# Attention with four score banks and early products in runs of twelve, and three expert chunks loaded through the later pool

## The chip, the core and the metric

The kernel runs as one program on one core of a Trainium2 chip. The metric is the device time of an execution in microseconds. The time of the kernel before is the median of three runs: 646.68 us (645.85 to 648.88).

The core has five engines with a queue each. TensorE (PE) multiplies matrices and writes only to PSUM, a memory of eight banks, each 128 partitions by 512 float32. ScalarE (ACT) and VectorE (DVE) read PSUM and work elementwise; GpSimd (POOL) works on SBUF only and issues gathers and scatters; SyncE (SP) issues most DMA transfers. An engine takes its instructions in the order of its queue, and waits at the first whose inputs are not there.

## The reference, cut to what matters

The computation is an attention with a window, a gated pair of products, and a layer of eight experts:

```python
# attention: q, k, v of (batch 2, heads 8, sequence 768, head dim 64)
scores = scale * np.matmul(q, k.transpose(0, 1, 3, 2))
keep = (pos[None, :] < n_sink) | ((rel >= 0) & (rel < window))   # n_sink 4, window 128
scores = np.where(keep, scores, -1e9)
a = np.exp(scores - scores.max(-1, keepdims=True))
a = a / (a.sum(-1, keepdims=True) + 1e-9)
x = np.matmul(a, v)                       # then as (1536 tokens, 512)
# gated product
x = ((x @ w_a) * (x @ w_b)) @ w_out       # w_a, w_b: 512 x 1536; w_out: 1536 x 512
# experts: each token goes to one of 8, at most 192 tokens per expert, best logits first
logits = x @ w_gate
for e in range(8):
    h = np.maximum(x[assigned == e] @ w1[e], 0.0)     # 512 x 1024
    out[assigned == e] = h @ w2[e]                    # 1024 x 512
```

## The kernel before, in words

**Exactness.** The products run in a float32 format of reduced mantissa (F32R). Where that is not enough, a value is split into a high part and the low rest, and a product becomes three: high by high, high by low, low by high. So xh and xl are the two parts of the attention's output, whi and wlo those of a weight, ehi and elo those of an expert's weight.

**Attention.** It is worked off in 24 steps (n = 0 to 23): two batches, three groups g of two query blocks each, four pairs of heads hp. The order of the instructions on PE, ACT, DVE and POOL is written out by hand: the framework adds the semaphores, but moves nothing on these four engines. One round of the loop in `attention` works on four steps at once:

- `turned` and `turned_low` (L231 to L255) turn k and q of step n+2 on PE into one bank; ACT writes the high part of T, DVE the low part.
- `scores` (L257 to L280) makes the scores of step n+1, in two groups j = 0, 1 of two heads. Each head has a bank of its own from a ring `s`, which has two (SB = 2). Three matmuls fill it; DVE reduces it with the mask (L277), ACT takes the exponential (L279).
- `factors`, `normed`, `sinks` (L282 to L317) norm the weights of step n, on DVE and POOL. Where g > 0, the eight sink columns are put into a tile AS of their own.
- `weights_turned` (L328) turns the weights of step n for each head, into a ring `at` of three banks; `sinks_turned` (L319) turns AS into the third bank of the same ring. Where g = 0 there are no sinks and `sinks_turned` does nothing.
- `copied` (L337), one round later, copies these banks to SBUF: the first head and the sinks (ast) on ACT, the second head on DVE.
- `values` (L352) multiplies them by v into one bank px, and ACT copies xh from it; `values_low` lets DVE write xl from px and xh.

Between these stand places 0 to 6, at each of which `fill` may put other work into the queues: idle matmuls (`busy`), the conversion of the first weights from 64-bit words (rounds 7 to 14, `PACE`), and **early products**. These are the gated products of the first two blocks of w_a and w_b with the first two thirds of the attention's output: eight banks, each the sum of twelve matmuls of 512 columns (L470), into one bank `pa` of a pool of its own, and evacuated by ACT (L476) or DVE (L478). `FILL` says how many stand at each place of a round: two at place 0, one at each of places 3 to 6, from round 9 on; what is left comes after the loop.

The order of a round on PE before: turn (n+2), two early products, scores j = 0 (n+1), values (n-1), scores j = 1 (n+1), one early product, weights (n) of the first head, one, of the second head, one, sinks (n), one. The eight PSUM banks are: `s` 2, turn 1, `at` 3, px 1, `pa` 1.

**After the attention** come the gated products (L559), the product with w_out (`second`, L977) with the routing of the tokens (`routing`) between its parts, and the experts. `second` makes twelve blocks of 128 tokens; each is stored to the DRAM tensor x2d by a DMA that ACT issues (L984), the last one stays in SBUF as x2last. `first_rows` (L1009) gathers the first expert's tokens from x2d by two DMAs of POOL (L1018); they must follow the eleventh store. PE turns the gathered rows (L1035), adds the rows of x2last (L1147), and starts the first expert (L1092).

**The experts' weights** come in 64 chunks of 512 KB, eight per expert, each loaded by a DMA of SP (`weight_load`, L997) into a tile eraw, from which ACT makes ehi and DVE elo. Chunks 0 to 3 are loaded into the pool `exraw` (three buffers) long before they are needed, and converted at the end of the routing. The later pool `more` (six buffers) lies in memory that `second` uses until its end. `load` (L1072) decides which pool a chunk takes; before, chunks below 7 take `exraw`. A chunk's load stands in SP's queue behind that of the chunk before.

Of the kernel before, what the change touches and what calls it, by code (L numbers as in the profile page):

```python
# [9 lines left out]
F32 = mybir.dt.float32  # L10
F32R = mybir.dt.float32r
# [6 lines left out]
PSUM = bass.MemoryType.PSUM  # L18
# [21 lines left out]
WARM = 12  # L40
BUSY = {(-2, 0): 7, (-1, 0): 1, (-1, 1): 1, (-1, 3): 1, (0, 0): 1, (0, 1): 1, (0, 3): 1, (2, 4): 3, (7, 0): 1}
CONV_IN = 2
FILL = (2, 0, 0, 1, 1, 1, 1)
FILL1 = (2, 0, 0, 1, 1, 1, 1)
PACE = (1, 1, 1, 0, 0, 0, 1)
ORDER = (0, 1, 0)
SINKV = (0, 2)
FIRST = (("q", 0, 0, 2), ("k", 0, 0, 2), ("q", 0, 2, 4), ("k", 0, 2, 4), ("v", 0, 0, 2), ("q", 0, 4, 8), ("k", 0, 4, 8),
         ("v", 0, 2, 4), ("q", 1, 0, 4), ("k", 1, 0, 4), ("v", 0, 4, 8), ("q", 1, 4, 8), ("k", 1, 4, 8), ("s", 0), ("v", 1))
# [1 line left out]
         8: (("w", 3),), 9: (("v", 3), ("s", 1), ("q", 4), ("k", 4)), 13: (("v", 4), ("q", 5), ("k", 5)), 14: (("v", 5),)}  # L51
CONV_AT = (7, 9, 11, 13)
CONV_ON = (0, 0, 0, 0, 1)
SB, ATB = 2, 3
SINK = 8
WB, AB, NB, FB = 4, 2, 1, 2
KB = 128 + SINK
# [6 lines left out]
def f32(ap):  # L64
    return ap.bitcast(F32)


class Kernel:
# [110 lines left out]
    def open_attention(self, ctx):  # L179
        tc = self.tc  # L180
        self.qkp = ctx.enter_context(tc.tile_pool(name="qkp", bufs=3))
        self.kt = ctx.enter_context(tc.tile_pool(name="kt", bufs=1))
        self.aw = ctx.enter_context(tc.tile_pool(name="aw", bufs=3))
        self.atps = ctx.enter_context(tc.tile_pool(name="atps", bufs=1, space=PSUM))
        self.raw, self.vb, self.T, self.vs, self.vraw = {}, {}, {}, {}, {}
        self.AS = [self.kt.tile([128, 2, 128], F32R, name=f"AS{n}") for n in range(3)]
        self.nAS = 0
        for AS in self.AS:
            self.nc.gpsimd.memset(f32(AS), 0.0)

    def busy(self, n):

        if n:
            p = self.abe.tile([128, 512], F32, name="none", tag="pa", bufs=1)
            for _ in range(n):
                self.nc.tensor.matmul(p[:, 0:256], self.idle[:, 0:128], self.idle[:, 0:256], start=True, stop=True)

# [59 lines left out]
    def scores(self, st, j):  # L257
        nc, b, g, hp = self.nc, st.b, st.g, st.hp
        i = 2 * g + j
        if j == 0:  # L260
            st.A2 = self.aw.tile([128, 2, 2, 256 + SINK], F32, name="A", tag="A", bufs=4)
            st.r2 = self.aw.tile([128, 2, 2], F32, name="rs", tag="rs", bufs=4)
        T = self.T[b, hp]
        flat = T.rearrange("p t k c -> p t (k c)")
        c0 = KB if i == 0 else 0
        lo, n = (0, 128) if i == 0 else (KB * (i - 1), 256 + SINK)
        mask = self.mask0 if i == 0 else self.mask1 if i == 1 else self.mask2
        col0 = ((b * 6 + i) * self.H) + 2 * hp
        for h in range(2):
            s = self.atps.tile([128, 256 + SINK], F32, name="s", tag="s", bufs=SB)  # L270
            hs = slice(64 * h, 64 * h + 64)
            for t, (tq, tk) in enumerate(((0, 0), (0, 1), (1, 0))):
                nc.tensor.matmul(s[:, :n], T[hs, tq, 6 + i % 2, 0:128], flat[hs, tk, lo:lo + n],  # L273
                                 start=(t == 0), stop=(t == 2))
            sm = self.aw.tile([128, 256 + SINK], F32, name="sm", tag="sm", bufs=4)
            cc = slice(col0 + h, col0 + h + 1)
            nc.vector.tensor_tensor_reduce(out=sm[:, :n], in0=s[:, :n], in1=mask, scale=-self.scale, scalar=BIG,  # L277
                                           op0=OP.add, op1=OP.min, accum_out=self.negmax[:, cc])
            nc.scalar.activation(st.A2[:, j, h, c0:], sm[:, :n], AF.Exp, bias=self.negmax[:, cc], scale=-1.0,  # L279
                                 accum_out=self.sums[:, cc])  # L280
# [38 lines left out]
    def sinks_turned(self, st):  # L319
        nc = self.nc  # L320
        if not st.g:
            return
        pt = self.atps.tile([128, 2, 128], F32R, name="pt", tag="at", bufs=ATB)
        for n in range(2):
            nc.tensor.transpose(pt[:, n, :], st.AS[:, n], self.identr)
        st.ps.append((pt[0:6 * SINK], None))
# [25 lines left out]
    def values(self, st):  # L352
        nc, D, b, g, hp = self.nc, self.D, st.b, st.g, st.hp
        i0 = 2 * g
        px = self.atps.tile([128, 512], F32, name="px", tag="px", bufs=1)[:, 0:256]
        if g:
            nc.tensor.matmul(px, self.vs[b][:, hp, :], st.ast.rearrange("p a b -> p (a b)"), start=True, stop=False,
                             skip_group_check=True)
        vcol = [slice((2 * hp + h) * D, (2 * hp + h + 1) * D) for h in range(2)]
        parts = [(i0, slice(0, 256), slice(1, 3))]  # L360
        if g:
            parts.append((i0 - 1, slice(0, 128), slice(0, 1)))
        parts.append((i0 + 1, slice(128, 256), slice(3, 4)))
        for n, (kb, cols, sl) in enumerate(parts):
            for h in range(2):
                vv = self.vb[b, kb].rearrange("p h d -> p (h d)")
                nc.tensor.matmul(px[64 * h:64 * h + 64, cols], vv[:, vcol[h]],  # L367
                                 st.AT[h][:, sl].rearrange("p a b -> p (a b)"),
                                 start=(not g and n == 0), stop=(n == len(parts) - 1), skip_group_check=True)
        st.px = px  # L370
        nc.scalar.activation(st.out[0][:, hp, :], px, AF.Copy)
# [2 lines left out]
        xh, xl = [x[:, st.hp, :] for x in st.out]  # L374
        self.nc.vector.tensor_tensor(xl, st.px, f32(xh), op=OP.subtract)

    def attention(self, XH, XL, wpool, GE, abe):

        steps = []
        for gi in range(6):  # L380
            b, g = divmod(gi, 3)
            cols = slice(256 * (gi % 2), 256 * (gi % 2) + 256)
            for hp in range(4):
                steps.append(SimpleNamespace(b=b, g=g, hp=hp, AT=[], ps=[],
                                             out=(XH[gi // 2][:, :, cols], XL[gi // 2][:, :, cols])))
        early = self.early(wpool, XH, XL, GE, abe)

        done, raw, under_way = [0], {}, {}

        def fill(n, place):  # L390
            self.busy(BUSY.get((n, place), 0))
            for i, n1 in enumerate(CONV_AT):
                if (n, place) == (n1, 0):
                    engs = [(self.nc.vector, self.nc.gpsimd)[e] for e in CONV_ON]
                    under_way[i] = self.split_steps(wpool, raw.pop(i), engs[:4], engs[4])
                if n >= n1 and i in under_way:
                    for _ in range(7 if (n, place) == (n1 + CONV_IN - 1, 6) else PACE[place]):
                        res = next(under_way[i], None)
                        if res:
                            self.ahead[i // 2].append(res)  # L400
                            del under_way[i]
                            break
            ready = 12 * sum((n, place) >= (max(8 * c + 8, n1 + CONV_IN), 2) for c in range(2) for n1 in CONV_AT)
            for _ in range(min((FILL if n < 17 else FILL1)[place], ready - done[0])):
                next(early)
                done[0] += 1

        for n in range(-2, len(steps) + 1):
# [7 lines left out]
            def norm():  # L416
                if this:
                    self.factors(this)
                    self.normed(this)
                    self.sinks(this)  # L420
                    if (this.g, this.hp) == SINKV:
                        self.sink_values(this.b)

            if ORDER[0] == 0:
                norm()
            if last:
                self.copied(last)
            if ORDER[0] == 1:
                norm()
            if after:  # L430
                self.turned(after)
            fill(n, 0)
            if then:
                self.scores(then, 0)
            if ORDER[0] == 2:
                norm()
            if after:
                self.turned_low(after)
            fill(n, 1)
            if last:  # L440
                self.values(last)
                if ORDER[1] == 0:
                    self.values_low(last)
            fill(n, 2)
            if then:
                self.scores(then, 1)
            if last and ORDER[1] == 1:
                self.values_low(last)
            fill(n, 3)
            if this:  # L450
# [6 lines left out]
        for _ in early:  # L457
            pass

    def early(self, wpool, XH, XL, GE, ps):  # L460

        nc = self.nc
        for c in range(2):
            for f in range(NE):
                res = []
                for m, (hi, lo) in enumerate(self.ahead[f]):
                    p = ps.tile([128, 512], F32, name="pa", tag="pa", bufs=1)
                    for k in range(4):
                        for t, (w, x) in enumerate(((hi, XH), (hi, XL), (lo, XH))):
                            nc.tensor.matmul(p, w[:, k, :], x[c][:, k, :], start=(k == 0 and t == 0),  # L470
# [98 lines left out]
    def run(self):  # L569
        tc, nc = self.tc, self.nc  # L570
        H, NT, E = self.H, self.NT, self.E
        with ExitStack() as top:
# [12 lines left out]
            XH, XL = [], []  # L585
# [3 lines left out]
            self.open_attention(att)  # L589
            for item in FIRST:  # L590
                self.load(*item)
            abe = self.abe = att.enter_context(tc.tile_pool(name="abe", bufs=1, space=PSUM, side="right"))
            self.ahead = {}
            self.busy(WARM)
            with tc.manual_schedule(engines=MANUAL):
                self.attention(XH, XL, wpool, GE, abe)
            att.close()

            gs = ExitStack()
# [438 lines left out]
    def experts(self, tag, exraw, trp, first=None, weights=None):  # L1038
# [5 lines left out]
        with tc.tile_pool(name="ex" + tag, bufs=2) as pool, tc.tile_pool(name="er" + tag, bufs=EXR2) as more, \  # L1044
# [26 lines left out]

            def load(c):  # L1072
                if c < 8 * E and c not in raws and c not in ready:
                    raws[c] = self.weight_load(exraw if weights and c < 7 else more, c)

            def high(s):

# [258 lines left out]
```

## Time and profile before

| | us |
|---|---|
| median of three runs | 646.68 |
| profiled execution | 648.35 |
| its span in the trace | 646.1 |
| PE busy | 620.3 (96%) |
| DVE busy | 404.0 (63%) |
| ACT busy | 337.3 (52%) |
| POOL busy | 175.9 (27%) |

The span is the time from the first to the last instruction of the program; the profiled execution's own time lies around it. The busy time of PE is a modelled one, since its matmuls overlap; where PE's instructions follow one another without a break, the distance between two starts or two ends tells more than the duration. In the chain that ended last, a piece is the time by which an instruction's end lies behind the end of the one before it. The attention lies before 132.7 us, the gated products reach to 329.6, the second product and the routing to 466.8, the experts to the end.

### The profile page before, as it was taken

The numbers are of one execution on the slowest core, as the hardware profiler recorded it, in microseconds if no ns is written. First come the engines' busy times: TensorE is split into PE (matmuls) and PEld (weight loads), VectorE is DVE, ScalarE is ACT, GpSimd is POOL, SyncE is SP. The second block draws the span as 40 slices with busy tenths as digits, with TensorE's granted clock in tenths as the row PEclk, the third lists the DMA queues.
The fourth block names the chain that finished last, engine by engine and source line by source line (L and its number), as shares of the span: only waits on it lengthen the run. The fifth ranks groups of instructions, "written<-read, shape, count | busy, mean of one in ns | idle before, by whom it ended". The sixth has DMA issues, their size and how long they took to land.

```text
span 646.1 us, 10265 instructions
## 1 busy us (share of the span) xinstructions
PE 620.3 (96%) x3705; PEld 491.2 (76%) x3705; DVE 404.0 (63%) x873; ACT 337.3 (52%) x669; POOL 175.9 (27%) x299
## 2 busy tenths in 40 slices
PE   7999999999999999999999999999869999999994
PEld 5767777778878888788866776677668888888883
DVE  5788876579966767342126556666207787777782
ACT  3788777644442334122126655663307666668671
POOL 5557664400000000001024344344321222232221
PEclk7999999999999999999999999999959999999997
DMA  7966310044542233200040000000381888787841
GB/s 161 219 123 159 66 67 2 2 129 133 164 130 77 88 98 98 66 0 1 0 131 17 18 33 17 34 17 33 119 281 26 276 253 260 257 245 231 259 144 34
DMA packets 82602, 72.16 MB, mean 112 GB/s; under 512 B 41072, under 2 KB 69744, under 8 KB 82544
## 3 DMA queue, kind: packets, MB, share of 16 engines
q1 hardware_dynamic: 78704, 61.99, 33.3%
q0 software_dynamic: 2112, 6.30, 3.0%
q10 hardware_dynamic: 1728, 3.15, 1.3%
q8 instruction: 31, 0.51, 0.3%
q14 instruction: 27, 0.22, 0.1%
HBM read 65.13 MB, written 6.29 MB: 111 GB/s over the span
## 4 chain that ended last, share of the span: by engine, by line
PE 80%; issue 9%; DVE 3%; DMA 2%; POOL 2%; ACT 1%; POOLq 0%; DVEq 0%; ACTq 0%
PE pa L559 14%; PE pb L559 14%; PE px L977 13%; PE p L1092 7%; PE pa L470 4%; PE s L273 4%; PE px L367 4%; PE pa L334 3%; POOL out_dram L1107 2%; PE pq L856 2%; PE pw L662 1%; PE pt L237 1%; DVE gt L845 1%; PE y L1098 1%; PE y L1099 1%
## 5 line engine op out<-in xcount | busy, mean ns | idle before, releaser
L1007 DVE TENSOR_TENSOR elo<-eraw,ehi 128x1024 fp32r<-128x1024 f32 x64 | 75.9, 1216 | 5.0 <-ACT ehi L1002 5.0
L1092 PE MATMUL p<-xt,ehi 128*128 128x384 f32 x256 | 73.6, 360 | 0.0
L963 POOL TENSOR_TENSOR gl<-G,gh 128x512 fp32r<-128x512 f32 (+1 forms) x40 | 47.9, 1206 | 71.5 <-ACT gh L962 71.5
L1002 ACT ACTIVATE ehi<-eraw 128x1024 fp32r<-128x1024 f32 x64 | 65.0, 1054 | 3.8 <-DVE oidx L932 2.3
L1092 PE MATMUL p<-xt,elo 128*128 128x192 f32 x256 | 64.7, 254 | 0.0
L977 PE MATMUL px<-woh,gh 128*128 128x512 f32 x144 | 59.9, 416 | 0.0
L279 ACT ACTIVATE A<-sm,negmax 128x264 f32<-128x264 f32 (+1 forms) x96 | 46.9, 490 | 23.6 <-DVE negmax L277 22.5
L963 POOL TENSOR_TENSOR gl<-GE,gh 128x256 fp32r<-128x256 f32 x8 | 7.1, 882 | 188.4 <-ACT gh L962 184.9
L845 DVE TENSOR_SCALAR gt<-lgT,vmax 128x1536 bf16<-128x1536 f32 x40 | 45.4, 1196 | 20.4 <-ACT lgT L820 17.7
L977 PE MATMUL px<-woh,gl 128*128 128x512 f32 x144 | 57.6, 400 | 0.0
L977 PE MATMUL px<-wol,gh 128*128 128x512 f32 x144 | 57.5, 399 | 0.0
L566 DVE TENSOR_TENSOR G<-asb,pb 128x512 f32<-128x512 f32 x32 | 21.9, 685 | 54.7 <-PE pb L559 54.7
L301 POOL TENSOR_SCALAR A<-A,rs 128x256 f32<-128x256 f32 (+1 forms) x96 | 43.2, 469 | 44.8 <-DVE rs L288 24.9
L559 PE MATMUL pb<-xh,whi 128*128 128x512 f32 x128 | 51.1, 399 | 0.0
L559 PE MATMUL pa<-xh,whi 128*128 128x512 f32 x128 | 50.9, 398 | 0.0
L1107 POOL DMA_INDIRECT out_dram<-o,oidx x16 | 26.3, 1645 | 90.2 <-ACT o L1116 68.2
L559 PE MATMUL pb<-xh,wlo 128*128 128x512 f32 x128 | 50.1, 391 | 0.0
L559 PE MATMUL pb<-xl,whi 128*128 128x512 f32 x128 | 50.0, 390 | 0.0
L559 PE MATMUL pa<-xh,wlo 128*128 128x512 f32 x128 | 49.9, 390 | 0.0
L1092 PEld LDWEIGHTS p<-xt,elo 128*128 128x128 f32 x256 | 49.4, 193 | 0.6 <-ACT xt L1069 0.2
L559 PE MATMUL pa<-xl,whi 128*128 128x512 f32 x128 | 49.8, 389 | 0.0
L1092 PEld LDWEIGHTS p<-xt,ehi 128*128 128x128 f32 x256 | 48.3, 189 | 0.7
(220 smaller groups left out, 1439.5 us busy)
## 6 DMA issues: line engine op xcount, KB each, us to landing
eraw<-in_moe_w_dram SPq DMA_DIRECT2D x64, 512.0 KB
wraw<-in_moe_w_a_dram SPq DMA_DIRECT2D x12, 512.0 KB
wraw<-in_moe_w_b_dram SPq DMA_DIRECT2D x12, 512.0 KB
wraw<-in_moe_w_out_dram SPq DMA_DIRECT2D x12, 512.0 KB
x2d<-x ACTq DMA_DIRECT2D x11, 256.0 KB
rawv<-in_v_dram SPq DMA_DIRECT2D x10, 256.0 KB
rawq<-in_q_dram SPq DMA_DIRECT2D x8, 256.0 KB
rawk<-in_k_dram SPq DMA_DIRECT2D x8, 256.0 KB
```

The source lines that it names most:

```text
L273: nc.tensor.matmul(s[:, :n], T[hs, tq, 6 + i % 2, 0:128], flat[hs, tk, lo:lo + n], start=(t == 0), stop=(t == 2))
L279: nc.scalar.activation(st.A2[:, j, h, c0:], sm[:, :n], AF.Exp, bias=self.negmax[:, cc], scale=-1.0, accum_out=self.sums[:, cc])
L301: nc.gpsimd.tensor_scalar(blocks, blocks, st.r2[:, j, h:h + 1], 1.0, op0=OP.mult, op1=OP.mult)
L367: nc.tensor.matmul(px[64 * h:64 * h + 64, cols], vv[:, vcol[h]], st.AT[h][:, sl].rearrange("p a b -> p (a b)"), start=(not g and n == 0), ...
L559: nc.tensor.matmul(pab[m], w[:, k, :], x[:, k, :], start=(k == 0 and t == 0), stop=(k == 3 and t == 2))
L845: nc.vector.tensor_scalar(gt, vrow, v, None, op0=OP.is_lt)
L963: nc.gpsimd.tensor_tensor(gl[:, fs], src, f32(gh[:, fs]), op=OP.subtract)
L977: nc.tensor.matmul(out[t], w[:, ff, :], x[f], start=(f == 0 and n == 0), stop=(f == 11 and n == 2))
L1002: self.nc.scalar.activation(hi, raw, AF.Copy)
L1007: (eng or self.nc.vector).tensor_tensor(lo, raw, f32(hi), op=OP.subtract)
L1092: nc.tensor.matmul(p1[:, ff, 0:c], w[:, k, cols], x[:, k, 0:c], start=(n == 0), stop=(k == 3), skip_group_check=True)
L1107: st = nc.gpsimd.indirect_dma_start(out=self.out, out_offset=bass.IndirectOffsetOnAxis(ap=self.oidx[:n, 2 * e + h:2 * e + h + 1], axis=0), ...
```

## The change

In the attention the ring `s` has four banks (SB = 4), `at` has two, and the pool of `pa` is gone: early products and idle matmuls take a bank of the ring `s`. The sinks are turned into the upper half of the bank px, which is now one tile that is made once; the values take its lower half, as before. Both score groups stand in one run, ahead of the values. Early products stand at place 3 only, twelve in a row (one whole bank), in odd rounds. Among the experts' chunks, those from 4 to 6 take the pool `more`.

The order of a round on PE after: turn (n+2), scores j = 0 and j = 1 (n+1), values (n-1), in odd rounds from 9 on twelve early products, weights (n) of both heads, sinks (n). On ACT the copy xh (n-1) stands behind all four exponentials of step n+1.

```diff
-FILL = (2, 0, 0, 1, 1, 1, 1)
-FILL1 = (2, 0, 0, 1, 1, 1, 1)
+RUN = 12
 PACE = (1, 1, 1, 0, 0, 0, 1)
-ORDER = (0, 1, 0)
...
-SB, ATB = 2, 3
+SB, ATB = 4, 2
...
+        self.px = self.atps.tile([128, 512], F32, name="px")
...
+    def bank(self):
+
+        return self.atps.tile([128, 512], F32, name="s", tag="s", bufs=SB)
+
     def busy(self, n):
...
-            p = self.abe.tile([128, 512], F32, name="none", tag="pa", bufs=1)
+            p = self.bank()
...
-            s = self.atps.tile([128, 256 + SINK], F32, name="s", tag="s", bufs=SB)
+            s = self.bank()
...
-        pt = self.atps.tile([128, 2, 128], F32R, name="pt", tag="at", bufs=ATB)
+        pt = self.px[:, 256:512].bitcast(F32R).rearrange("p (i q) -> p i q", i=2)
...
-        px = self.atps.tile([128, 512], F32, name="px", tag="px", bufs=1)[:, 0:256]
+        px = self.px[:, 0:256]
...
-            for _ in range(min((FILL if n < 17 else FILL1)[place], ready - done[0])):
+            for _ in range(min(RUN if place == 3 and n % 2 else 0, ready - done[0])):
                 next(early)
                 done[0] += 1
...
             if then:
                 self.scores(then, 0)
...
             fill(n, 1)
+            if then:
+                self.scores(then, 1)
+            fill(n, 2)
             if last:
                 self.values(last)
-                if ORDER[1] == 0:
-                    self.values_low(last)
-            fill(n, 2)
-            if then:
-                self.scores(then, 1)
-            if last and ORDER[1] == 1:
                 self.values_low(last)
             fill(n, 3)
...
-                    p = ps.tile([128, 512], F32, name="pa", tag="pa", bufs=1)
+                    p = self.bank()
...
-                    raws[c] = self.weight_load(exraw if weights and c < 7 else more, c)
+                    raws[c] = self.weight_load(exraw if weights and c < len(weights) else more, c)
```

`weights` holds the four chunks converted beforehand, so `len(weights)` is 4.

## Rows read from the trace of the kernel before

**Rows 1.** chain that ended last, no early products: start us, us, engine, tile

```profile
...
34.80 1.02 PE px L367 x12
...
39.17 1.02 PE px L367 x12
...
44.50 0.60 DVE T L252
...
50.83 1.02 PE pa L334 x8
...
```

**Rows 2.** the same chain, steps with early products and the end of the attention

```profile
...
99.81 0.56 PE s L273 x6
...
100.49 1.02 PE px L367 x12
...
102.07 0.42 PE pa L470
...
103.85 0.12 PE pt L325 x2
...
104.28 0.44 PE pt L237 x4
...
111.23 1.02 PE px L367 x12
...
132.73 2.72 PE pa L559 x12
...
```

**Rows 3.** the same chain at the start of the experts

```profile
...
461.98 5.07 DMA eraw<-in_moe_w_dram
...
474.30 3.97 PE pt L1035 x16
...
481.12 9.92 PE p L1092 x64
...
```

**Rows 4.** POOL in order of time; in brackets idle before and releaser

```profile
...
467.04 1.16 POOL L1018 DMA_INDIRECT first<-x2d,idx  x1 [3.94 <-DMA eraw<-in_moe_w_dram]
468.50 0.97 POOL L1018 DMA_INDIRECT first<-x2d,idx  x1 [0.30 <-issue]
...
```

**Rows 5.** busy PE, PEld, DVE, ACT, POOL by stage; clock, DMA share, GB/s

```profile
...
466.80:481.10 14.30, 6.80 (x26) 6.46 (x26) 0.56 (x1) 1.07 (x2) 5.87 (x6) 0.57 0.95 303
...
```

**Rows 6.** DVE in order of time, one step of the attention

```profile
...
36.40 0.43 DVE L277 CUSTOM_DVE_ANT_0 sm<-s,mask 128x264 f32<-128x264 f32 x1 [0.42 <-PE s L273]
...
36.76 0.43 DVE L277 CUSTOM_DVE_ANT_0 sm<-s,mask 128x264 f32<-128x264 f32 x1
...
37.12 0.42 DVE L375 TENSOR_TENSOR xl<-px,xh 128x256 fp32r<-128x256 f32 x1
...
```

**Rows 7.** PE in order of time, sinks' transposes after a wait

```profile
...
46.73 0.36 PE L325 MATMUL pt<-identr,AS 128*128 128x128 f32 x2 [0.53 <-POOL AS L317]
...
```

**Rows 8.** ACT in order of time, the same step as rows 6

```profile
...
36.13 0.36 ACT L371 ACTIVATE xh<-px 128x256 fp32r<-128x256 f32 x1
36.88 0.52 ACT L279 ACTIVATE A<-sm,negmax 128x264 f32<-128x264 f32 x1 [0.38 <-DVE negmax L277]
...
37.39 0.50 ACT L279 ACTIVATE A<-sm,negmax 128x264 f32<-128x264 f32 x1
...
```

**Rows 9.** SP's DMA issues in order of time

```profile
...
466.89 0.37 SPq L997 DMA_DIRECT2D eraw<-in_moe_w_dram  x1
```

**Rows 10.** ACT's DMA issues in order of time, the stores to x2d

```profile
...
449.97 0.33 ACTq L984 DMA_DIRECT2D x2d<-x  x1
...
461.34 0.33 ACTq L984 DMA_DIRECT2D x2d<-x  x1
...
```

**Rows 11.** DMA from 449 to 453, busy tenths in 0.1 us slices

```profile
...
DMA  0000000000000000008989997100000000000000
...
```

**Rows 12.** DMA from 465 to 466, queue of the stores: packets, MB, share

```profile
...
q10 hardware_dynamic: 9, 0.01, 3.8%
...
```

**Rows 13.** all that touches x2d from 485 to 530 us: the gathers' landing

```profile
...
DMA to landing us min/median/max: 3.0/3.3/3.5
```

More of the change, by code (lines that the diff above doesn't have):

```diff
@@ L375, in values_low, with attention @@
         self.nc.vector.tensor_tensor(xl, st.px, f32(xh), op=OP.subtract)
-    def attention(self, XH, XL, wpool, GE, abe):
+    def attention(self, XH, XL, wpool, GE):
         steps = []
@@ L385, in attention @@
                                              out=(XH[gi // 2][:, :, cols], XL[gi // 2][:, :, cols])))
-        early = self.early(wpool, XH, XL, GE, abe)
+        early = self.early(wpool, XH, XL, GE)
         done, raw, under_way = [0], {}, {}
@@ L422, in norm @@
                         self.sink_values(this.b)
-            if ORDER[0] == 0:
-                norm()
+            norm()
             if last:
                 self.copied(last)
-            if ORDER[0] == 1:
-                norm()
             if after:
@@ L434, in attention @@
                 self.scores(then, 0)
-            if ORDER[0] == 2:
-                norm()
             if after:
@@ L458, in attention, with early @@
             pass
-    def early(self, wpool, XH, XL, GE, ps):
+    def early(self, wpool, XH, XL, GE):
         nc = self.nc
@@ L591, in run @@
                 self.load(*item)
-            abe = self.abe = att.enter_context(tc.tile_pool(name="abe", bufs=1, space=PSUM, side="right"))
             self.ahead = {}
@@ L595, in run @@
             with tc.manual_schedule(engines=MANUAL):
-                self.attention(XH, XL, wpool, GE, abe)
+                self.attention(XH, XL, wpool, GE)
             att.close()
```

## The prediction

> **What bounds the kernel now.** I read the chain of waits first, then the instructions of single engines in order of time over the two places that the change touches, then the DMA. TensorE ends nearly every link, so a change pays where TensorE waits or does needless work.
>
> In the attention there are two kinds of step, and the chain tells them apart. Without early products a step lasts 4.37 us (34.80 to 39.17 [rows 1]), although TensorE's own work in it is about 3.8 (turn 0.44, scores 2 x 0.56, sink and value products 1.13, weights turned 1.02, sinks turned 0.12 [rows 1, 2]). With early products nothing in the chain is anything but TensorE, and two steps take 100.49 to 111.23, 10.74 us [rows 2].
>
> The second place is the start of the experts. TensorE ends the second product near 466.8 and waits until 474.30 for a gather that POOL issues at 467.04 [rows 3, 4]. The granted clock over 466.8 to 481.1 is 0.57 [rows 5], so the 6.8 us of small matmuls behind the gather run mostly at the lower of its two levels, and the first expert's products begin at 481.12 [rows 3].
>
> **Attention: TensorE's work.** The first score group of a run costs 0.56 us, of which some 0.2 is the change to matmuls on half the rows: six of 264 columns, two at a time, would be 0.33 [rows 2]. With four banks the second group follows at once, so a run of twelve is about 0.56 + 0.33 = 0.9, against 1.12 in two places. Early products cost 2.72 for twelve in a row and 0.42 for the first one after scores [rows 2]; twelve in one place are 2.72 + 0.2 = 2.9. A pair of steps then needs: turns 2 x 0.44, scores 2 x 0.9, sink and value products 2 x 1.13 (0.11 between the scores' end and px, and 1.02), early products 2.9, weights turned 0.88 behind the early products and 1.02 in the other step, sinks turned 2 x 0.12 [rows 1, 2]. That is 10.0 against 10.74. If TensorE alone set the pace, eight pairs would give back some 5.5 us.
>
> **Attention: the new wait.** It does not set the pace alone. The sinks' transposes now write the upper half of the bank px, whose lower half ACT (xh) and DVE (xl) still read. No row of before shows two engines on halves of one bank. I take it that the write waits for xl of the same step, since both halves are views of one tile made once. What is queued behind it on TensorE is everything of the next step. And xh now stands behind four exponentials on ACT, where it stood behind two. The Trainium skill, PSUM — Partial Sum Buffer, section "PSUM bank collisions raise a hardware error", says that two engines must not touch one bank and quadrant at once, whatever the columns, and that software must order them. By that rule the wait exists; no trace here shows it.
>
> The loop is then xl, sinks turned, the next turn, scores, reductions, exponentials, xh, xl. By rows: xl 0.42, sinks turned after a release 0.36 and some 0.05 to start [rows 6, 7], turn 0.44, first score group 0.56 and 0.04, two reductions 2 x 0.36, low part of T 0.60, from the third reduction's start to its exponential 0.48, two exponentials 0.51 + 0.50, xh 0.36 and 0.04 to xl [rows 1, 2, 6, 8]. The sum is 5.1 us. A step without early products goes from 4.37 to 5.1; there are five with or before sinks (n = 4 to 8): **+3.5**.
>
> In a pair with early products the odd step has slack, since twelve products stand before its sinks. The even one has none. From the last early product: weights turned 0.88, sinks 0.12, turn 0.44, scores 0.60, reductions and T 1.32, 0.48, exponentials 1.01, xh 0.40, xl 0.42, sinks 0.41: 6.1 us. Then turn 0.44, scores 0.9, values 1.13, early products 2.9: 11.5 for the pair, **+0.75**. Five pairs have sinks in the even step (n = 10, 16, 18, 20, 22): **+3.8**. Two have none (n = 12, 14); there the 0.7 of TensorE's work is saved, and about half is lost to the second copy of at, which DVE now does after xl: -0.4 each, **-0.8**. Before, early products stood behind the last values, up to 132.73 [rows 2], and others covered the last copies; after n = 23 none is left, and TensorE waits for these: **+0.6**, my estimate from the links copy and px. Attention: **+7.1**.
>
> If the two halves are not ordered, the sinks don't wait: a pair is some 10.6, a step without early products 4.4, the tail as above, together about +1. The other end is 2 more than my sum, since DVE's weight conversions (n = 7 to 14) lie on the new loop in part. So the attention lies between -5.5 and +9. Three changes I cost at nothing. Two buffers for the turned weights in place of three: with sinks each step used three, so a buffer came back after one step then as now. The early products' bank, which the fourth score of the next step needs: its evacuation (0.6 to 0.7 on ACT or DVE) lies beside 0.88 + 0.12 + 0.44 of TensorE; without that cover it costs 0.6 a pair. GE's product on DVE ahead of the next factors: POOL's norming has the 3.5 us of the list above until TensorE needs it. The idle matmuls that now take score banks: nobody reads them, so nothing waits for their banks.
>
> **Experts: chunks four to six.** Moving them looks like a loss of prefetch, since the last of them is issued at 461.98 [rows 3], and all will be from about 466.9 on, when the first load of the later pool is issued [rows 9]. But the profile's releaser for the gather is misleading: it names that load [rows 3, 4], which the gather doesn't read. What it reads is x2d, whose last store but one is issued at 461.34 [rows 10], into those loads. A store of the same size in quiet, issued at 449.97, is over at 451.8 [rows 10, 11]; this one still has packets after 465 [rows 12]. Without the loads it ends at about 463.2. POOL is free from 463.1 on (3.94 idle before 467.04 [rows 4]), and the gather can be issued 2.5 us earlier, at 464.5. It then has the engines to itself until the loads start: in quiet a gather lands 3.0 to 3.5 us after issue [rows 13], here 7.2 [rows 3, 4]. So its halves land at 467.8 and, issued 1.46 later [rows 4], 469.0. TensorE waits 1 us, not 7.5. If the clock stays at the upper level, the 6.8 us take some 3.4, of which 1.0 can run before 469.0; the first expert's products begin at 471.4 instead of 481.12: **-9.7**. Bounds: 0, when the gather gains nothing, and -10.5.
>
> Chunk four is then needed by ACT after the first quarter of these products, near 473.7. At the 303 GB/s of [rows 5] a chunk of 512 KB takes 1.7 us, so four to six land by about 473, in this order; if the first were late, TensorE would wait only at the second products, 9.9 us after 471.4 [rows 3]. The later chunks find the same six buffers, in the same turn, and behind the moved loads SP's queue holds nothing but them.
>
> **Sum.** +7.1 - 9.7 = -2.6 us, against the profiled execution's 648.35 (span 646.1 and 2.25 around it): 645.75. That execution lies 1.67 above the median of 646.68, to which the same difference gives **644.1**.
>
> **Rivals.**
> - *The halves are not ordered* (or xl comes early enough): attention +1, experts -9.7, so 638. For it: the halves share no column. Against: one tile. 0.15.
> - *TensorE sets the pace throughout*: -5.5 - 9.7 gives 631.5. For it: no link of another engine in the steps with early products [rows 2]. Against: xh behind four exponentials. 0.1.
> - *The gather lands no sooner for being issued sooner*: its packets meet the six loads from 466.9 on, it again takes 7.2, TensorE waits until 471.7 and the clock falls as before. The gain is 2.5, and with the attention's 7.1 the time is 651.3, slower than before. It decides when the second gather's packets begin after 467.5, because POOL issues it later than 466. For it: before, the gather was that slow among the same loads. Against: the issue moves ahead of them. 0.18.
> - *The wrong reading of the gather's wait*: if it waits for something else until 467.04, there is no gain and 653.8; this is the far end of the last one, 0.05.
>
> **Chances.** My forecast has 0.52, within it some 640.5 to 648, from the size of the attention's wait (two steps' worth either way). Range 636 to 651: it leaves out the second rival, the last, and part of the third. A measurement of this kernel can tell about 0.5%, 3.2 us, from no change; so faster means under 643.4, slower over 649.9. Faster: nearly half of the forecast (0.24) and the first two rivals, 0.49. Slower: the last two for the most part, 0.16. The same: 0.35.
>
> **What would show it.** Right: sinks' transposes that wait for DVE's xl by 1 us and more in the steps without early products and in the even ones; pairs of 11.5 and steps of 5.1; L559's first matmul about 7 us later than 132.73; the gather some 2.5 us before the end of the second product, TensorE's wait for it near 1 us, and a granted clock of 1.0 through the first expert. Wrong: pairs near 10 or 10.6 (no such wait), or a gather that still takes 7 us and a clock that still falls; a first expert that waits for a load of chunk four.

## The result, and the profile after

The changed kernel takes **652.81 us** (median of 8 runs, 650.79 to 655.17); the kernel before, beside it, 647.70 (8 runs). The ratio is **1.0082, 95% interval 1.0056 to 1.0108**: slower, where 644.1 was forecast, and outside the range. The profiled execution took 655.0, span 652.7; its mean granted clock was 0.974, and runs at 0.986 to 0.989 took 650.8 to 653.1.

From the page of after, the busy times:

```profile
PE 619.4 (95%) x3705; PEld 492.9 (76%) x3705; DVE 402.7 (62%) x873; ACT 339.6 (52%) x669; POOL 175.7 (27%) x299
```

The span grew by 6.6 us, TensorE's busy time not at all. Where it went, by the starts and ends of TensorE's matmuls (the executions start up to 3 us apart, so the attention counts from its first value products to the first gated product):

| us | before | after | difference | forecast |
|---|---|---|---|---|
| attention | 113.9 | 127.4 | +13.5 | +7.1 |
| gated products | 197.1 | 198.0 | +0.9 | 0 |
| second product's end to the first expert product | 13.9 | 6.4 | -7.5 | -9.7 |
| experts, to the last matmul | 156.3 | 156.1 | -0.1 | 0 |

The wait that was forecast is there. TensorE's waits in the attention (engine and line that waited, whom for: us in total, times, longest):

```profile
PE px L329 <- DVE rs L291: 10.5, 8, 2.5
PE px L329 <- DVE xl L379: 1.9, 1, 1.9
PE pa L556 <- DVE xl L379: 0.9, 1, 0.9
```

L329 turns the sinks. L291 is DVE's next instruction after xl (L379): its event is the one by which xl is known to be done. The third wait stands ahead of the first gated product, so it belongs to the attention's row. One pair of steps in the chain of after, against [rows 2]:

```profile
108.56 0.87 PE pa L338 x8
109.43 0.13 PE px L329 x2
...
110.60 0.43 DVE sm L281
...
111.39 0.60 DVE T L256
112.00 0.34 DVE sm L281
...
112.38 0.38 ACT A L283
...
112.80 0.68 ACT A L283 x3
113.48 0.28 ACT xh L375
...
113.78 0.42 DVE xl L379
...
114.36 0.34 PE px L329 x2
...
117.22 2.95 PE s L467 x12
...
121.04 0.13 PE px L329 x2
```

From the last early product (108.56) to the end of the even step's sinks (114.70) it is 6.14 us; the pair, 109.43 to 121.04, is 11.61. The prediction had 6.1 and 11.5, each link right to about 0.1 us.

What it did not have is the clock. Windows of after (busy PE, PEld, DVE, ACT, POOL; then granted clock, DMA share, GB/s):

```profile
97.50:99.40 1.90, 0.00 (x0) 0.00 (x0) 1.56 (x5) 1.49 (x6) 0.66 (x2) 1.00 0.00 0
99.40:106.20 6.80, 6.28 (x34) 4.85 (x35) 3.98 (x16) 3.87 (x12) 2.60 (x8) 0.50 0.01 4
...
111.00:145.90 34.90, 29.48 (x247) 23.22 (x247) 19.21 (x71) 20.56 (x63) 13.72 (x41) 1.00 0.01 1
...
485.10:488.50 3.40, 3.40 (x12) 3.17 (x12) 0.63 (x2) 0.98 (x2) 1.07 (x2) 0.50 1.06 408
```

TensorE stands still from 97.5 on, behind the sinks; at 99.4 the granted clock goes from 1.00 to 0.50, the lower of its two levels, and stays there for 6.8 us of work. It did so at 34.6 and 51.6 too, 3.4 us each, behind waits of 1.57 and 1.87 us; in the profiled attention of before it did not. What made the 97.5 wait the longest stands in DVE's list (start, duration, in brackets idle before):

```profile
95.66 0.42 DVE L515 TENSOR_SCALAR wf<-wraw 128x512 int32<-128x512 int32 x1
...
97.30 0.75 DVE L517 SCALAR_TENSOR_TENSOR wf<-wraw,wf 128x512 int32<-128x512 int32 x1
97.97 0.42 DVE L281 CUSTOM_DVE_ANT_0 sm<-s,mask 128x264 f32<-128x264 f32 x1
...
98.32 0.68 DVE L519 SCALAR_TENSOR_TENSOR wf<-wraw,wf 128x512 int32<-128x512 int32 x1
99.35 0.42 DVE L379 TENSOR_TENSOR xl<-px,xh 128x256 fp32r<-128x256 f32 x1 [0.34 <-ACT xh L375]
```

Three steps of a weight's conversion stand between the reductions and ahead of xl. The first two (L515, L517) delay the reductions that the exponentials and xh wait for. The third (L519) costs nothing, since xl then still waits 0.34 us for xh.

At the experts the gathers are issued as forecast, 2.3 us before the second product's end at 480.98 (POOL, against [rows 4]):

```profile
478.68 1.16 POOL L1014 DMA_INDIRECT first<-x2d,idx  x1 [1.35 <-issue]
480.14 0.97 POOL L1014 DMA_INDIRECT first<-x2d,idx  x1 [0.30 <-issue]
```

And the chain around them, against [rows 3]:

```profile
475.57 2.02 DMA x2d<-x
...
480.14 3.79 DMA first<-x2d,idx
...
483.98 1.10 PE pt L1031 x8
485.08 2.47 PE pt L1143 x7
```

The store to x2d that the gather waits for now lands 2.0 us after its issue. The gathers land 3.5 and 3.8 us after theirs, TensorE waits 1.28 and 0.56 us, and the last tile's matmuls (L1143) fall into the half clock of 485.1.

### The profile page after: what moved, and what is told of

Read it like the earlier page. It is cut to its first block, busy times and chain, and to the rows that moved or that the text cites. A ratio compares the mean times of both kernels' runs of the same rounds, so it can differ in the third digit from the quotient of the medians.

```text
span 652.7 us, 10224 instructions
## 1 busy us (share of the span) xinstructions
PE 619.4 (95%) x3705; PEld 492.9 (76%) x3705; DVE 402.7 (62%) x873; ACT 339.6 (52%) x669; POOL 175.7 (27%) x299
## 4 chain that ended last, share of the span: by engine, by line
PE 66%; DVE 11%; issue 10%; DMA 4%; ACT 4%; POOL 3%; POOLq 0%; DVEq 0%; ACTq 0%; SPq 0%
PE px L973 13%; PE pb L556 11%; PE pa L556 10%; PE p L1088 7%; PE s L467 3%; ACT A L283 3%; PE s L277 3%; DVE sm L281 2%; POOL out_dram L1103 2%; PE pq L852 2%; DMA wraw<-in_moe_w_out_dram 2%; PE px L371 2%; PE pt L241 2%; DVE gt L841 1%; PE y L1094 1%
## 5 line engine op out<-in xcount | busy, mean ns | idle before, releaser
L959 POOL TENSOR_TENSOR gl<-G,gh 128x512 fp32r<-128x512 f32 (+1 forms) x40 | 47.9, 1206 | 70.9 <-ACT gh L958 70.9
```

What stands on the lines that cost most here:

```text
L959: nc.gpsimd.tensor_tensor(gl[:, fs], src, f32(gh[:, fs]), op=OP.subtract)
```

## The experiments

| kernel | us | ratio to before, 95% | attention | wait at experts |
|---|---|---|---|---|
| before | 647.7 to 649.1 | | 113.9 | 13.9 |
| after | 652.81 | 1.0082 [1.0056, 1.0108] | 127.4 | 6.4 |
| loads only | 640.81 | 0.9878 [0.9834, 0.9921] | 114.3 | 6.6 |
| attention only | 659.69 | 1.0173 [1.0137, 1.0208] | 125.1 | 15.1 |
| sinks apart, three banks | 651.80 | 1.0051 [1.0026, 1.0076] | 124.3 | 6.4 |
| three banks | 655.50 | 1.0103 [1.0080, 1.0126] | 128.7 | 6.0 |
| idle matmuls | 650.09 | 1.0027 [1.0002, 1.0052] | 123.4 | 6.2 |
| **xh before exps** | **640.30** | **0.9875 [0.9847, 0.9903]** | **112.2** | **5.4** |
| the same, loads undone | 647.14 | 0.9965 [0.9945, 0.9986] | 112.2 | 13.9 |
| two places | 654.58 | 1.0103 [1.0056, 1.0150] | 126.7 | 6.3 |
| twelves in before | 654.34 | 1.0088 [1.0055, 1.0122] | 121.3 | 13.7 |
| spread | 654.18 | 1.0070 [1.0044, 1.0096] | 125.3 | 7.4 |
| loads and idle | 640.07 | 0.9867 [0.9835, 0.9898] | 114.0 | 6.1 |

The last two columns come from one profiled execution each; that of xh before exps, 636.53 us, is the fastest of its five, the others took 640.1 to 640.6. "Wait at experts" runs from the second product's end to the first expert product. The kernel before was timed anew beside each group of runs, so times of different groups are better compared by their ratios.

**The two parts, each alone.** Before with the loads' line of the change, and after with it undone:

```diff
-raws[c] = self.weight_load(exraw if weights and c < 7 else more, c)
+raws[c] = self.weight_load(exraw if weights and c < len(weights) else more, c)
```

> The kernel before with one edit: chunks 4 to 6 take the later pool. My theory (the loads held up the store to x2d that the first gather waits for): about 7.5 us faster than before, 640; the gather is issued some 2.3 us before the second product ends, the first expert's products begin about 6.5 us after that end and not 13.9. Rival (the gather waits for something else, and the changed kernel's earlier start comes from its shifted attention): no change, 647.5.

> The changed kernel with chunks 4 to 6 back in the earlier pool, so the attention's change alone. My theory: the attention costs about 13 us in a trace (L556 begins near 146, against 132.6 before) and this kernel takes about 660. Rival (the parts are not additive, the attention's loss is regained elsewhere): 653 or less.

Both came as my theory had them. The loads gain 7.2 us, the attention loses 11.7; 648.0 - 7.2 + 11.7 is 652.5, against 652.81 for the changed kernel, so the parts add. The window of the wait at the experts, loads only:

```profile
465.88:472.51 6.63, 4.53 (x24) 4.27 (x25) 0.20 (x1) 1.09 (x2) 0.55 (x2) 0.84 0.90 312
```

The mean clock of 0.84 says that part of the stretch is still at half clock with the loads moved; with the attention alone it is 0.65 over 15.07 us.

**The sinks out of px.** They go back into the ring `at`, which costs a score bank; the control takes the bank and leaves the sinks in px.

```diff
-SB, ATB = 4, 2
+SB, ATB = 3, 3
...
-        pt = self.px[:, 256:512].bitcast(F32R).rearrange("p (i q) -> p i q", i=2)
+        pt = self.atps.tile([128, 2, 128], F32R, name="pt", tag="at", bufs=ATB)
```

> The changed kernel with the sinks turned into a third bank of the ring at, as before, for which the score ring has three banks instead of four. Theory A (the sinks' write waits for xh and xl on the other half of px): the waits of the sinks' transposes for DVE vanish, pairs of steps with early products fall from 11.6 to about 10.7, steps without from 4.8 to 4.4, the clock stays up in the attention, and the time falls by 8 to 12 us, to 641 to 645. Theory B (early products in odd steps only leave the even ones uncovered, whatever bank the sinks use): the wait moves to another instruction of the even step and the time stays within 3 us of 652.8.

> After, with three score banks and three buffers for the turned weights, the sinks still in px: the control of the run with the sinks apart, which had to take a score bank. If three banks cost by themselves (the last score matmuls of a run wait for the first group's reductions): slower than after by 2 to 6 us, 654 to 659, and the sinks' own place was worth 3 to 7. If the three banks cost nothing: 651 to 653, and the wait at the sinks, taken away alone, gave 1 us.

Waits of TensorE with the sinks apart, then in the control:

```profile
PE s L277 <- DVE negmax L281: 8.5, 18, 1.5
```

```profile
PE s L277 <- DVE negmax L281: 5.5, 18, 0.8
PE px L329 <- DVE rs L291: 5.4, 8, 1.3
PE px L329 <- DVE xl L379: 1.8, 2, 1.2
```

The time came as theory B had it, although the sinks' waits are gone as in theory A: others, at the score matmuls (L277), took their place. By the first run alone the sinks' place seemed worth 1 us. The control shows two effects that hide each other. The missing fourth bank lengthens steps with early products from 6.48 us to 7.2, since the run waits for the first group's reductions. The sinks' own bank shortens steps without from 5.15 to some 4.35 (ends of the turns of k and q: 110.84, 115.99 and 123.18 in the control, 108.41, 112.75 and 119.95 with the sinks apart). So the place is worth 0.8 us in such a step, 4.4 over the attention (128.7 to 124.3; less than ten times 0.8, since the sinks-apart kernel waits up to 1.5 us at L277 and had one fall of the clock) and 3.7 in the medians (655.5 to 651.8). The fourth bank's 2.7 in the medians (655.5 to 652.81) is not clear of noise, since the two intervals overlap. By the attention at the full clock it is worth more, 128.7 - 123.4 = 5.3 us: the control had no fall of the clock, after had three, and 123.4 is that of the next run, which has after's order and no fall.

**The clock alone.** Ten idle matmuls stand ahead of each of the turns of the sinks that waited.

```diff
+                self.busy(IDLE if this.g and (n < 9 or n % 2 == 0) else 0)
                 self.sinks_turned(this)
```

> The changed kernel with ten idle matmuls (bf16, 256 columns, results unused) ahead of the sinks' transposes in the rounds where these wait (n = 4 to 8 and even n). Theory A (the waits let the granted clock fall to its lower level, and that is a second cost beside the waits): the clock stays at 1.00 through the attention, and the kernel is 3 to 5 us faster than the changed one, 648 to 650. Theory B (the clock's fall is met by waits anyway and costs nothing): within 1 us of 652.8, or slower by the idle matmuls.

The window of its whole attention:

```profile
19.30:142.70 123.40, 117.12 (x1009) 91.76 (x1007) 85.27 (x311) 88.59 (x272) 66.29 (x173) 1.00 0.37 80
```

The clock is 1.00 throughout. A step without early products is still 5.15 and the one that follows it 6.48, since DVE's xl sets them, but the attention is 127.4 - 123.4 = 4.0 us shorter: that is the clock's part in the profiled execution. The attention-only kernel has after's order too and no idle matmuls: its clock was at 0.50 for 6.8 us of the attention (from 33.7 and from 98.6, 3.4 us each), after's for 13.7, and its attention, 125.1 us, lies between 123.4 without a fall and 127.4. In the medians the idle matmuls gain 2.7 us, by the two ratios 3.6 us; 650.09 is at the upper end of theory A.

**xh ahead of the second group's exponentials.** TensorE's order stays. The reductions and exponentials of a group are split from its score matmuls, so that on ACT xh is behind two exponentials, as in before, and not behind four. On DVE xl stays behind all four reductions; only single steps of the weights' conversion change places beside them.

```diff
             if then:
                 self.scores(then, 1)
             fill(n, 2)
             if last:
                 self.values(last)
+            if then:
+                self.reduced(then, 1)
+            if last:
                 self.values_low(last)
```

> After, with TensorE's order untouched; on ACT and DVE the second score group's reductions and exponentials stand behind xh and ahead of xl, so that xh is behind two exponentials and not four. Theory A (the sinks' wait for xl sets the step): xh and xl come earlier by up to an exponential or two, 0.5 to 1 us, in nearly every step; the waits of the sinks' transposes nearly vanish, fewer falls of the granted clock, 642 to 647 us. Theory B (twelve early products in one round and one score run in each make a longer step whichever wait ends it): the wait shows up at another place, 649 to 653 us.

> The attention of the run with xh ahead of the second group's exponentials (its first values to the gated products' start: 112.2 us, before 113.9), with the experts' chunks four to six loaded as before. If the two parts add, and the attention's edit is worth 1.7 us once ACT's order is mended: 646 to 648 us against 648 to 649 of before, no faster than can be told. If the short attention makes the gather later against the loads, as it did by 1.2 us in the run of the attention's edit alone, 648 to 650.

The median of 640.30 is below theory A's range. In the traces this one order on ACT takes 15.2 us out of the attention, 4.0 of them the clock's. The chain in a pair, and TensorE's waits:

```profile
97.98 1.02 PE pa L346 x8
...
99.09 0.33 PE px L337 x2
99.43 0.46 PE pt L241 x4
99.89 0.95 PE s L279 x12
100.84 0.11 PE px L369
100.94 1.02 PE px L379 x12
101.96 2.04 PE s L479 x8
```

```profile
PE px L337 <- DVE xl L387: 3.1, 2, 1.7
PE px L369 <- ACT ast L355: 1.3, 2, 0.9
```

No other engine is in the chain of the pair: 3.97 + 6.49 = 10.46 us (ends of the sinks 95.46, 99.43, 105.92), where before needs 10.74. The waits of 1.7 and 1.4 us that are left stand in the rounds with conversion steps on DVE. No fall of the clock is left in the attention or at the experts. This version beats both kernels. Its attention part alone gives 647.14, as expected, and 0.9965, interval 0.9945 to 0.9986: the edits that failed gain about 2 us once ACT's order is mended, 1.7 in the trace. On top of the loads' edit that gain does not show in the medians: 0.9875 here, 0.9878 for the loads only.

**Is it the run, or the twelve?** Three kernels were to tell these apart: after with the second score group behind the values; before with nothing but the early products in twelves, at place 3; after with the early products spread.

```diff
             if last:
                 self.values(last)
                 self.values_low(last)
             fill(n, 2)
+            if then:
+                self.scores(then, 1)
```

> After, with the second score group put back behind the values, as before; four score banks, the sinks in the upper half of px and twelve early products at every other round stay. Theory A (the run of both groups puts xh behind four exponentials): pairs near 11 us, steps without early products near 4.5, 643 to 647 us. Theory B (the twelve in one round cost, not the score run): unchanged, 650 to 653 us.

```diff
-            for _ in range(min((FILL if n < 17 else FILL1)[place], ready - done[0])):
+            for _ in range(min(12 if place == 3 and n % 2 else 0, ready - done[0])):
```

> Before, with the early products twelve in a row at the end of every other round, in their own bank; nothing else of the change. Theory A (the wait at the sinks is the whole loss): 645 to 649 us, pairs of 10.7 or less, since fewer short runs save TensorE a little. Theory B (bunching costs by itself: a step without early products is 4.4 us whoever sets it, and the step with twelve is that and 2.7): pairs of 11.3, the attention 3 to 4 us longer, 650 to 653 us.

```diff
-SB, ATB = 4, 2
+SB, ATB = 3, 2
...
-            for _ in range(min(RUN if place == 3 and n % 2 else 0, ready - done[0])):
+            for _ in range(min(FILL[place], ready - done[0])):
...
-                    p = self.bank()
+                    p = self.atps.tile([128, 512], F32, name="pa", tag="pa", bufs=1)
```

> After, with the early products six in every round at the places of before, in a bank of their own (three score banks left); xh stays behind four exponentials and the sinks in px. If the twelve in one round are half of the loss (the waits of the rounds without them have nothing to fill them): pairs back to 10.8, steps without early products unchanged near 5, 646 to 649 us. If the order on ACT is all of it: pairs of 11.3 and more, 650 to 654.

Two places gives 654.58, outside the ranges of both theories. There the values wait, not the sinks. TensorE's waits, and then the chain from xh to the values:

```profile
PE px L361 <- ACT ast L347: 8.6, 10, 1.6
PE px L371 <- ACT at L353: 3.2, 4, 0.9
```

```profile
111.74 0.42 DVE xl L379
112.16 0.34 DVE sm L281
...
113.65 0.48 ACT at L353
114.13 0.28 ACT ast L347
...
114.45 0.38 PE px L361
```

With the score groups apart, the second group's exponentials come late on ACT, and the copies `at` and `ast` that the next values need stand behind them. But this kernel does not put back the order of before: its xl stands on DVE ahead of the second group's reductions, where before has it behind them [rows 6], and xl and the wait for xh lie in the chain. So it does not show what undoing the run alone would give. The chain of twelves in before shows the same place:

```profile
107.12 0.48 ACT at L349
107.60 0.27 ACT ast L343
...
107.92 0.38 PE px L357
```

In before that wait lay under the six early products that stand between a round's second score group and the next round's values; bunched, they leave it bare in every other round. A pair of steps takes 11.26 us (as theory B had it, ends of the turns 103.24 and 114.50) and the attention 7.4 more; the time is above both theories' ranges. Some 1 us of the 7.4 (an estimate, from 4.0 us for 13.7 at the half clock) is a fall of the clock that came earlier, which the last section shows. So twelve in a row do cost with the old order. In the spread kernel the pairs are 11.8 (two steps of 5.9), no shorter, but three banks are in it: its score runs wait 3.8 us at L277 and its sinks 5.1 at L329. It doesn't tell the spread from the banks. So these three leave open what the run and the twelve cost each. What holds are the runs that differ in ACT's order (and in the conversion step's place): with the run, the twelve and the sinks in px all kept, it decides between 652.81 and 640.30, and without the loads' edit between 659.69 and 647.14.

**The clock at the experts.** Loads only, with 12 idle matmuls between the second product and the turns of the gathered rows:

```diff
+                for _ in range(IDLE):
+                    nc.tensor.matmul(pts[0][:, 0, 0:128], self.ident, self.ident, start=True, stop=True,
+                                     skip_group_check=True)
                 for h in range(2):
                     for k in range(4):
                         self.begin_rows(pts[k // 2][:, k % 2, :], rows, h, k)
```

> Before with the loads' edit alone, and 12 idle matmuls (of the identity, into the bank that the gathered rows' transposes overwrite) between the second product and these transposes, 1.3 us at the upper clock, in TensorE's wait for the first gather. If the granted clock falls there since TensorE idles: no fall near 470, the 2.6 us of matmuls of the last tile take 1.3, 1 to 1.5 us off the loads' edit alone, 638.5 to 640. If it falls for another reason, or the wait for the second gather (0.8 us) does it too: the same 640.8.

```profile
467.68:473.77 6.09, 6.09 (x49) 5.62 (x48) 0.02 (x1) 1.09 (x2) 0.13 (x1) 1.00 0.90 299
```

The clock stays at 1.00 and the stretch is 0.5 us shorter than 6.63, where 1 to 1.5 was expected; in the medians, 640.07 against 640.81, the difference can't be told from none. The twelve took 2.68 us and not 1.3, so the first turns began 1.3 us after the first gather had landed. From the second gather's landing to the first expert product it is 2.9 us here and 3.4 with loads only; three kernels without a fall there (xh before exps, three banks, two places) take 2.6.

## Why the prediction was wrong, step by step

- *The sinks' transposes wait for xl:* right, and the loop was sized right: 6.14 us against 6.1, a pair of 11.61 against 11.5. Three banks against sinks apart shows 0.8 a step for it.
- *The attention's sum, +7.1:* the step that failed, in two ways. First, **it is a sum at a constant clock.** At the experts the prediction wrote "if the clock stays at the upper level", having seen 0.57 there [rows 5]; in the attention it added ten waits of some 1 us to TensorE and did not ask the same. The clock's part is 4.0 us (idle matmuls). Second, the sizes: at the full clock the attention is still 9.4 us over before, beyond even the +9 that the prediction gave as the far end. Up to the sinks of n = 8 it is 3.9 (forecast 3.5). From there to the sinks of n = 23 it is 4.1 (before's last nine early products counted with it), where 3.8 - 0.8 was forecast: the pairs without sinks saved 0.2 in all and not 0.8, and the step at n = 16, with conversion steps on DVE in its loop, took 5.95 us (the one at n = 7, 5.88) where the others without early products take 5.15. The prediction had named such conversions, for n = 7 to 14, as part of its far end, and not added them. The tail is 1.4 (forecast 0.6): TensorE waits 0.47 us for the last copy and 0.94 for the last xl.
- *Nothing for the gated products:* they take 0.9 us more. TensorE waits once, 0.75 us at 191.9, for DVE's wp; before has no such wait, and no run shows why DVE is later there.
- *Experts, -9.7:* the reading of the gather's wait was right (loads only); the issue came 2.3 us ahead of the second product's end, as said, and no chunk was missed. It gave -7.5, and three sizes make up the 2.2 us of the miss, to within 0.1. The second gather landed 3.0 us after the second product's end and not 2.2. The clock did fall: from that landing to the first expert product it is 3.5 us, and 2.6 in the three kernels without a fall. And the split of the rows on ACT and DVE ahead of the first product was not counted, 0.6 us between the last of these matmuls and the first expert product (468.98 to 469.61 in the chain of xh before exps).
- *Rivals:* that the gather lands no sooner fell (3.5 and 3.8 us, not 7.2). That the halves are not ordered fell: the sinks' waits for xl go when the sinks leave px. Whether it is the shared tile or the shared bank that orders them stays open, since no run has two tiles in one bank. "TensorE sets the pace throughout", at 631.5, was given 0.1 as a forecast for this kernel; it is nearly the state that one order on ACT brings about, 640.30, 12.5 us below the changed kernel. But there TensorE's pair takes 10.46 us, where the prediction's sum for TensorE alone was 10.0, so that the attention gives back 1.7 us and not 5.5.
- *The sum:* 13.5 + 0.9 - 7.5 - 0.1 is 6.8 us, the 6.6 of the span to within 0.2 that lie outside these rows and in rounding. The medians differ by 5.1: the profiled execution of after lies 2.2 us above its median, that of before 0.7 above the median of 647.70.

## What to carry to other kernels

When work on TensorE is moved, follow what it feeds on the other engines: here the second score group moved ahead of the values dragged two exponentials ahead of the copy xh, and with it of xl, which the sinks' write waits for; putting back that one order turned 1.0082 into 0.9875. When an edit adds waits to TensorE, price them twice, as waits and as a possible fall of the granted clock behind them. And when an experiment has to pay for what it takes away (a bank), run the payment alone as its control: "1 us" was a gain of 0.8 us in each step without early products less a loss of 0.7 in each step with them.

## What was not expected of the hardware

- A wait of 2.46 us before 99.92 was followed by 6.8 us at a granted clock of 0.50 (it fell at 99.4, within the wait), and two steps, between ends of the turns, took 15.30 us (94.71 to 110.01) where idle matmuls took 12.42 (94.40 to 106.82).
- The same waits do not always bring a fall. With three banks TensorE waited 12.7 us in all at L277 and L329, none longer than 1.3 us, and the whole attention ran at 1.00. Twelves in before fell, for 3.4 us from 47.9, behind waits of 0.53 and 0.73 us, ahead of its first early product and so where its code is that of before; before has the same two waits there and did not fall. The two windows, three banks first:

```profile
19.45:148.10 128.65, 114.07 (x907) 88.39 (x906) 85.12 (x309) 88.40 (x270) 66.20 (x172) 1.00 0.36 77
```

```profile
47.90:51.30 3.40, 3.40 (x22) 2.47 (x23) 1.72 (x8) 2.01 (x7) 3.34 (x9) 0.51 0.27 70
```

Sinks apart (from 52.4) and two places (from 52.9) had one such fall each, although their sinks hardly wait. So which wait brings a fall stays open, and new waits are not the only thing that does. What the runs show is the price, and that with idle matmuls in the waits the profiled attention had no fall.
